# First output piece with its relu terms ahead of its weight-product terms, and state sums that VectorE decays kept in PSUM

## The chip, the cores and the metric

The kernel runs on one core of one Trainium2 chip. The metric is the device time of one execution in microseconds (us), taken as the median over runs. Engines are called TensorE (PE in the profile, PEld for its weight loads), VectorE (DVE), ScalarE (ACT), GpSimd (POOL) and SyncE (SP, which issues all DMAs here).

## The reference

Two stages. A gated linear attention over 4 batches, 8 heads, 768 tokens, head dimension 48:

```
f = 1 / (1 + exp(-f_logit))
for t in range(S):
    state = f[t, :, None] * state + outer(k[t], v[t])      # 48 x 48 per batch and head
    y[t] = q[t] @ state
```

Then, with x the 3072 x 384 matrix of all y rows (heads side by side), a maxout layer: `out = maximum(x @ w1, x @ w2) @ w_out`, with w1 and w2 of 384 x 1024 and w_out of 1024 x 384. Inputs and output are f32.

## The kernel before, in words

**Tiling.** The 3072 rows are cut into 12 windows s = 0 to 11 of 256 tokens; window s belongs to batch s % 4 and is that batch's window number s // 4. A window lies on 128 partitions with two neighbouring tokens (even and odd) on each. Its lower and upper 64 partitions are its halves h = 0 and 1, of 128 tokens each. The recurrence is worked out chunk by chunk: inside a half by a masked product of decayed q and k, and from half to half by a 48 x 48 state per head, kept in bf16 in the tiles `st0` to `st3` (one per batch).

**The steps of a window.** E, F and G (ScalarE) turn f_logit into logs of the gates; e (line 202) adds even and odd; C (lines 206, 209) makes cumulative sums on TensorE; X and Z (ScalarE, lines 216, 221) make `inv` and `dec` from them; i, j, K and Q (lines 225, 229, 236, 239) decay k and q; V casts v; t and u transpose k and q on TensorE (line 256) and U copies them to SBUF (`trs`); A (line 273) makes the products and m masks them; S (line 313) adds what the previous states give and y (lines 313, 341) what the window itself gives; Y casts the result to `xT`. z (line 329) reads two elements, so that what follows is ordered after S.

**The state.** D (line 357) sums k times v of each half into one PSUM bank per half (`sadd`, 128 x 192 f32). Step n (lines 370 to 375) handles a half that has a state before it by adding that state to the sums, into the SBUF f32 tile `tmp_s` (three buffers in rotation); step N (line 378) then multiplies `tmp_s` by the decay (a slice of `dec`, spread over 48 columns) and writes the new state. A half with no state before it (half 0 of windows 0 to 3) takes one multiplication straight from PSUM (line 375). N runs on GpSimd for 14 of its 16 uses, and on VectorE for half 0 of window 5 (N5.0) and of window 10 (N10.0).

**The maxout layer.** It is computed as relu(x (w1 - w2)) w_out + x (w2 w_out). `wd` is w1 - w2 (line 482); `m2` is the product w2 w_out, in three row blocks: TensorE products wm (line 472), stored by wn (line 476, helper line 103). d (line 396) multiplies `xT` by `wd` into PSUM, r (lines 405, 407) takes the relu into `gT`, and o (lines 412 to 421) makes one output piece of 128 rows (the even or the odd tokens of a window; in the last window the odd piece is cut in two): first three terms `xT` x `m2` (line 417), then eight terms `gT` x `wo` (line 420), accumulated in one PSUM bank. b copies a piece to SBUF; O and P store.

**The order of the work** is written out by hand in the string `ORDER` (lines 20 to 54): one word per step, with the window, the piece or half, the engine (a ScalarE, v VectorE, p GpSimd, s SyncE) and the PSUM bank after @. Every engine takes its words in that order; semaphores between engines follow from what the steps read and write. The words around the change:

```
... wm0@7 E2 r0.1v@4 ... wm2@6 E3 e2p wn0v@7 wm1@4 ... j2v wn2a@6 e3p C2@7 wn1v@4 d1.3@1 ... i2v o0.0@6 Z2 K2v
... Q2v t2@4 r1.1a@0 D2@2 Lf4s@10 u2@4 ...
... A5.0@0 D5@2 X7 N4.1p z4 o3.0@5 n5.0v Z7 N5.0v E6 Q7p Lq8s@2
n5.1v m5.0v@0 E8 S5@2 y4 b3.0a@5 ... A5.1@0 F6 o3.1@5 m5.1v@0 Y4a@6 e6p
... D10@5 A10.1@0 z11 n10.0v y11 N10.0v m10.1v@0 S10@2 o9.1@5 ...
```

The first output piece is o0.0. The states that the change touches are made by n5.0v and N5.0v, which S5 reads, and n10.0v and N10.0v, which S10 reads.

Of the kernel before, what the change touches and what calls it, by code (L numbers as in the profile page):

```python
# [11 lines left out]
F32 = mybir.dt.float32  # L12
# [7 lines left out]
ORDER = """  # L20
# [37 lines left out]
def kernel(  # L58
# [14 lines left out]
    nc = tc.nc  # L73
    B, H, S, D = q.shape
    C = 128
# [3 lines left out]
    NP = H // 2  # L79
# [3 lines left out]
    FG = d_ff // C  # L83
    KT = HD // C
    n_s = nw * B
    places = [(x, h, x * DP - h * D) for x in range(2 * KT) for h in range(H)
              if x * DP < (h + 1) * D and h * D < (x + 1) * DP]

    consts = ctx.enter_context(tc.tile_pool(name="consts", bufs=1))
    inp = ctx.enter_context(tc.tile_pool(name="inp", bufs=1))  # L90
    work = ctx.enter_context(tc.tile_pool(name="work", bufs=2))
# [85 lines left out]
    wo = consts.tile([C, FG, HD], BF16, name="wo")  # L177
    m2 = consts.tile([C, KT, HD], BF16, name="m2")
# [8 lines left out]
    gate, ell, one, cum, inv, dec, tr, at_b, at, states, sadd, tmps = ({} for _ in range(12))  # L187
# [99 lines left out]
    def has_state(s, h):  # L287
        return s >= B or h > 0

    def state_before(s, h):  # L290
        return states[s][:, 0] if h else states[s - B][:, 1]
# [70 lines left out]
    def decay(s, h):  # L362
        return dec[s][:, HD:].rearrange("p (j h) -> p j h", h=2)[:, :, h:h + 1].to_broadcast([C, NP, D])

    def state_of(s):
        if s not in states:
            states[s] = pad(f"st{s % B}", s)
        return states[s]

    def step_n(s, h):  # L370
        if has_state(s, h):
            tmps[s, h] = work.tile([C, NP, D], F32, name="tmp_s", tag="tmp_s", bufs=3)
            nc.vector.tensor_add(tmps[s, h], sadd[s][h][:, :, 0:D], state_before(s, h)[:, 1::2, :])  # L373
        else:
            nc.vector.tensor_mul(state_of(s)[:, h, 1::2, :], sadd[s][h][:, :, 0:D], decay(s, h))

# [4 lines left out]
    xT, gT, obs = {}, {}, {}  # L381
# [6 lines left out]
    def x_flat(s):  # L388
        return xT[s].rearrange("p k a h t -> p k (a h t)")
# [19 lines left out]
    def piece(g, i):  # L409
        return (i, slice(0, HD)) if i == 0 or g < n_s - 1 else (1, (slice(0, 2 * C), slice(2 * C, HD))[i - 1])  # L410

    def step_o(g, i, b):
        par, m = piece(g, i)
        cols = slice(par * C, (par + 1) * C)
        ps = banks[:, b, m]
        for kt in range(KT):
            nc.tensor.matmul(out=ps, lhsT=x_flat(g)[:, kt, cols], rhs=m2[:, kt, m],  # L417
                             start=(kt == 0), stop=False)
        for ff in range(FG):
            nc.tensor.matmul(out=ps, lhsT=gT[g][:, ff, cols], rhs=wo[:, ff, m],  # L420
                             start=False, stop=(ff == FG - 1))

    def step_b(g, i, e, b):
        par, m = piece(g, i)
# [54 lines left out]
    def subtract(q, e):  # L479
# [20 lines left out]
        "Y": lambda s, e, b: step_Y(s, e, b),  # L500
        "D": lambda s, e, b: step_D(s, b),
        "n": lambda s, i, e, b: step_n(s, i), "N": lambda s, i, e, b: step_N(s, i, e),
        "d": lambda s, i, e, b: step_d(s, i, b), "r": lambda s, i, e, b: step_r(s, i, e, b),
        "o": lambda s, i, e, b: step_o(s, i, b), "b": lambda s, i, e, b: step_b(s, i, e, b),
        "O": lambda s, e, b: step_O(s), "P": lambda s, i, e, b: step_P(s, i, e),
        "wc": lambda i, e, b: cast_w2(i, e), "wt": lambda i, e, b: transpose_w2(i, b),
# [1 line left out]
        "wm": lambda i, e, b: m2_product(i, b), "wn": lambda i, e, b: store_m2(i, e, b),  # L508
        "ws": lambda i, e, b: subtract(i, e),
    }  # L510
    for word in ORDER.split():
        key, of, e, b = re.fullmatch(r"([A-Za-z]+)([0-9.]+)([avps]?)@?([0-9]*)", word).groups()
        steps[key](*map(int, of.split(".")), e, int(b or 0))

# [29 lines left out]
```

## Time and profile before

| | us |
|---|---|
| median of 3 runs | 141.15 |
| lowest, highest | 140.92, 141.65 |
| the profiled execution | 141.12 |
| its span, first to last instruction | 139.3 |

| engine | busy us | share of the span |
|---|---|---|
| TensorE | 122.4 | 88% |
| VectorE | 99.6 | 72% |
| ScalarE | 83.1 | 60% |
| GpSimd | 56.6 | 41% |

The granted TensorE clock was 1.000 over the span. Matmuls overlap their neighbours in these records: a group's printed end is modelled and lies up to 0.2 us behind the start of the next group where TensorE runs without a stop. The printed idle time before an instruction is counted from that end. A wait is put down to the engine and line whose semaphore came last.

### The profile page before, as it was taken

Reading aid. Unit: us, or ns where it says so; the run is one execution under the profiler, and the core shown is the slowest. Engines: PE = TensorE matmul, PEld = TensorE weight load, DVE = VectorE, ACT = ScalarE, POOL = GpSimd, SP = SyncE. Lnnn points to the kernel's source line nnn. Section 1 sums busy time; section 2 is a strip of 40 time slices with the busy share of each in tenths; the row PEclk is TensorE's granted clock in tenths of the full one; section 3 lists DMA queues with packets and bytes.
Section 4 is the critical chain, followed back from the end, with each engine's and each line's share of the span. In section 5 each row is a group of like instructions: output and inputs, shape, how many; then the busy total and the mean of one; then the engine's idle time right before and its main releaser. Section 6 shows DMA issues by size and latency. Waiting matters only on the chain.

```text
span 139.3 us, 5772 instructions
## 1 busy us (share of the span) xinstructions
PE 122.4 (88%) x2575; PEld 91.6 (66%) x2575; DVE 99.6 (72%) x155; ACT 83.1 (60%) x119; POOL 56.6 (41%) x64
## 2 busy tenths in 40 slices
PE   0026699999899999996999999999999999999991
PEld 0024677876567788665688657886678876778670
DVE  5778968756988787789778686967957689643130
ACT  3646464769677679796578687978126470404400
POOL 7604519526188795736601382530860501000000
PEclk9999999999999999999999999999999999999999
DMA  4999999999999999999999999891113000032014
GB/s 112 271 261 264 374 386 378 334 257 238 274 266 239 256 268 274 273 263 253 292 316 273 244 260 292 239 319 50 59 59 118 0 5 7 5 132 98 3 53 169
DMA packets 54617, 28.68 MB, mean 206 GB/s; under 512 B 50240, under 2 KB 51648, under 8 KB 54592
## 3 DMA queue, kind: packets, MB, share of 16 engines
q1 hardware_dynamic: 54592, 28.32, 76.7%
q8 instruction: 20, 0.33, 1.0%
q14 instruction: 5, 0.04, 0.1%
HBM read 23.59 MB, written 4.72 MB: 203 GB/s over the span
## 4 chain that ended last, share of the span: by engine, by line
PE 79%; DMA 9%; DVE 3%; POOL 3%; SPq 2%; ACT 2%; issue 1%; DVEq 0%; POOLq 0%
PE banks L396 23%; PE banks L420 21%; PE banks L417 9%; DMA slots<-in_moe_w_dram 6%; PE banks L341 5%; PE banks L256 4%; PE banks L273 4%; PE banks L313 4%; PE banks L472 3%; DMA slots<-in_f_logit_dram 3%; POOL wd L482 3%; PE banks L357 2%; PE banks L206 2%; DVE st L378 1%; SPq L114 1%; SPq L125 1%
## 5 line engine op out<-in xcount | busy, mean ns | idle before, releaser
L420 PE MATMUL banks<-wo,gT 128*128 128x384 bf16 (+2 forms) x200 | 35.3, 320 | 0.0
L396 PE MATMUL banks<-xT,wd 128*128 128x256 bf16 x288 | 34.6, 274 | 0.3 <-POOL wd L482 0.3
L281 DVE TENSOR_TENSOR at_m<-banks,mask 128x1024 bf16<-128x1024 f32 x24 | 28.7, 1218 | 6.0 <-PE banks L273 6.0
L396 PEld LDWEIGHTS <-wd 128*128 128x128 bf16 x288 | 27.3, 98 | 4.5 <-POOL wd L482 0.6
L420 PEld LDWEIGHTS <-gT 128*128 128x128 bf16 x200 | 19.3, 98 | 12.0
L405 ACT ACTIVATE gT<-banks 128x1024 bf16<-128x1024 f32 x16 | 16.0, 1022 | 9.5 <-PE banks L396 9.2
L239 POOL TENSOR_TENSOR qp<-slots,dec 128x768 bf16<-128x768 f32 x8 | 15.1, 1888 | 11.4 <-ACT dec L221 6.0
L103 ACT COPY ob<-banks 128x384 f32<-128x384 f32 (+2 forms) x18 | 9.0, 501 | 16.8 <-PE banks L420 14.1
L378 POOL TENSOR_TENSOR st<-tmp_s,dec 128x192 bf16<-128x192 f32 x14 | 7.9, 566 | 23.6 <-DVE tmp_s L373 21.4
L417 PE MATMUL banks<-m,xT 128*128 128x384 bf16 (+2 forms) x75 | 16.1, 321 | 0.4 <-DVE m L103 0.4
L407 DVE TENSOR_SCALAR gT<-banks 128x1024 bf16<-128x1024 f32 x8 | 9.7, 1222 | 5.7 <-PE banks L396 5.3
L191 ACT ACTIVATE gate<-slots 128x768 f32<-128x768 f32 x12 | 10.0, 845 | 4.6 <-DMA slots<-in_f_logit_dram 4.6
L103 DVE COPY ob<-banks 128x384 f32<-128x384 f32 (+2 forms) x11 | 5.9, 542 | 8.5 <-PE banks L420 8.1
L103 DVE COPY trs<-banks 128x2048 bf16<-128x2048 bf16 x8 | 9.7, 1220 | 3.0 <-PE banks L256 3.0
L341 PE MATMUL banks<-at_m,vb 64*64 64x128 bf16 x576 | 11.7, 224 | 0.0
L103 ACT CAST xT<-banks 128x768 bf16<-128x768 f32 x8 | 6.4, 798 | 8.8 <-PE banks L341 8.7
L225 POOL TENSOR_TENSOR slots<-slots,one 128x384 f32<-128x384 f32 x7 | 7.6, 1084 | 9.8 <-ACT one L199 6.4
L273 PE MATMUL banks<-trs 48*64 48x128 bf16 x384 | 9.6, 234 | 1.3 <-DVE trs L103 1.3
L313 PE MATMUL banks<-trs,st 48*64 48x128 bf16 x240 | 8.7, 227 | 2.2 <-DVE look L329 1.1
L195 ACT ACTIVATE ell<-gate 128x768 f32<-128x768 f32 x12 | 10.1, 843 | 0.6
L236 DVE TENSOR_TENSOR kp<-slots,inv 128x768 bf16<-128x768 f32 x9 | 8.6, 963 | 2.6 <-issue 1.4
L206 PE MATMUL banks<-e,u_inc 128*128 128x384 bf16 x12 | 4.3, 356 | 6.8 <-DVE e L202 6.8
(64 smaller groups left out, 180.1 us busy)
## 6 DMA issues: line engine op xcount, KB each, us to landing
slots<-in_f_logit_dram SPq DMA_DIRECT2D x12, 384.0 KB, 6.3
slots<-in_k_dram SPq DMA_DIRECT2D x12, 384.0 KB, 6.4
slots<-in_q_dram SPq DMA_DIRECT2D x12, 384.0 KB, 6.2
slots<-in_v_dram SPq DMA_DIRECT2D x12, 384.0 KB, 6.1
out_dram<-ob SPq DMA_DIRECT2D x11, 384.0 KB, 5.4
slots<-in_moe_w_dram SPq DMA_DIRECT2D x4, 768.0 KB, 9.1
slots<-in_moe_w_out_dram SPq DMA_DIRECT2D x2, 768.0 KB, 13.6
out_dram<-ob SPq DMA_DIRECT2D x1, 192.0 KB, 1.9
```

The costliest lines, as they stand in the source:

```text
L103: (nc.scalar.copy if e == "a" else engines[e].tensor_copy)(out, in_)
L191: nc.scalar.activation(flat(gate[s]), flat(loaded[s]["f"]), AF.Exp, bias=0.0, scale=-1.0)
L195: nc.scalar.activation(flat(ell[s]), flat(gate[s]), AF.Ln, bias=1.0, scale=1.0)
L239: engines[e].tensor_mul(pad("qp", s)[:, :, :, 0:D], by_parity(loaded[s]["q"]), both(dec[s][:, 0:HD].rearrange("p (h d) -> p h d", h=H)))
L273: nc.tensor.matmul(out=ps[h * HC:(h + 1) * HC, j % 2, par, :], lhsT=t[rows, h, 0, j, par, :], rhs=t[rows, h, 1, j].rearrange("p a t -> p ( ...
L281: nc.vector.tensor_mul(at[s][:, jj].rearrange("p r j a t -> p (r j) (a t)"), banks[:, b:b + 2, :].rearrange("p r (j x) -> p (r j) x", j=2) ...
L313: nc.tensor.matmul(out=ys[s][h][cols, kt, :], lhsT=window(state_before(s, h)[rows], head // 2, off), rhs=tr[s][rows, h, 1, head // 2].rear ...
L341: nc.tensor.matmul(out=ys[s][h][cols, kt, :], lhsT=window(vb[rows, par], head, off), rhs=m[rows, head // 4, head % 2, head // 2 % 2, par, ...
L396: nc.tensor.matmul(out=ps[:, f, :], lhsT=wd[:, kt, ff * C:(ff + 1) * C], rhs=x_flat(g)[:, kt, :], start=(kt == 0), stop=(kt == KT - 1))
L405: nc.scalar.activation(dst, src, AF.Relu)
L417: nc.tensor.matmul(out=ps, lhsT=x_flat(g)[:, kt, cols], rhs=m2[:, kt, m], start=(kt == 0), stop=False)
L420: nc.tensor.matmul(out=ps, lhsT=gT[g][:, ff, cols], rhs=wo[:, ff, m], start=False, stop=(ff == FG - 1))
```

## The change

In the output piece that comes first in `ORDER` (o0.0) the eight relu terms are issued before the three `m2` terms; all other pieces keep their order. Where N runs on VectorE (N5.0 and N10.0), step n writes its sum over the sums in PSUM, instead of into `tmp_s`, and N multiplies from there. `ORDER` itself, and so the order of the steps on each engine, is the same. The rotation of the three `tmp_s` buffers skips these two uses.

```diff
+    words = ORDER.split()
...
     def step_n(s, h):
         if has_state(s, h):
-            tmps[s, h] = work.tile([C, NP, D], F32, name="tmp_s", tag="tmp_s", bufs=3)
-            nc.vector.tensor_add(tmps[s, h], sadd[s][h][:, :, 0:D], state_before(s, h)[:, 1::2, :])
+            sums = sadd[s][h][:, :, 0:D]
+            tmps[s, h] = sums if f"N{s}.{h}v" in words else work.tile([C, NP, D], F32, name="tmp_s", tag="tmp_s", bufs=3)
+            nc.vector.tensor_add(tmps[s, h], sums, state_before(s, h)[:, 1::2, :])
...
+    first_o = tuple(map(int, re.search(r"\bo(\d+\.\d+)", ORDER).group(1).split(".")))
+
     def step_o(g, i, b):
...
-        for kt in range(KT):
-            nc.tensor.matmul(out=ps, lhsT=x_flat(g)[:, kt, cols], rhs=m2[:, kt, m],
-                             start=(kt == 0), stop=False)
-        for ff in range(FG):
-            nc.tensor.matmul(out=ps, lhsT=gT[g][:, ff, cols], rhs=wo[:, ff, m],
-                             start=False, stop=(ff == FG - 1))
+        terms = [(x_flat(g)[:, kt, cols], m2[:, kt, m]) for kt in range(KT)]
+        relu = [(gT[g][:, ff, cols], wo[:, ff, m]) for ff in range(FG)]
+        terms = relu + terms if (g, i) == first_o else terms + relu
+        for n, (x, w) in enumerate(terms):
+            nc.tensor.matmul(out=ps, lhsT=x, rhs=w, start=(n == 0), stop=(n == KT + FG - 1))
```

More of the change, by code (lines that the diff above doesn't have):

```diff
@@ L510 @@
     }
-    for word in ORDER.split():
+    for word in words:
         key, of, e, b = re.fullmatch(r"([A-Za-z]+)([0-9.]+)([avps]?)@?([0-9]*)", word).groups()
```

## The prediction

> **What bounds the kernel now.** I read the page first, then the waits of TensorE, then the chain of waits around the two places that the change touches, and last the timeline there.
>
> ```profile
> PE 122.4 (88%) x2575; PEld 91.6 (66%) x2575; DVE 99.6 (72%) x155; ACT 83.1 (60%) x119; POOL 56.6 (41%) x64
> ...
> PE 79%; DMA 9%; DVE 3%; POOL 3%; SPq 2%; ACT 2%; issue 1%; DVEq 0%; POOLq 0%
> ```
>
> The chain that ended last is 79% TensorE, and in time order it holds nothing but TensorE from 64.64 us to 136.24 us. A microsecond gained on TensorE before 64.64 therefore comes out at the end, unless something that does not move with TensorE is late behind it. TensorE's list of waits is short, and after 24 us only two entries of it are left, both at places of this change:
>
> ```profile
> PE banks L313 <- DVE tmp_s L373: 1.0, 1, 1.0
> PE banks L417 <- DVE m L103: 0.4, 1, 0.4
> ```
>
> The first is S5, which waits for window 5's state; the second is the first output piece, which waits for the second block of `m2`. The chain around S5, as start, length, what:
>
> ```profile
> 61.45 0.32 PE banks L357 x32
> ...
> 61.83 0.37 DVE tmp_s L373
> ...
> 62.23 1.88 DVE st L378
> ...
> 64.23 0.37 DVE tmp_s L373
> 64.60 0.04 issue
> 64.64 0.53 PE banks L313 x24
> ```
>
> The sums D5 (L357) end, VectorE adds (n5.0, 0.37), decays (N5.0, 1.88), adds the other half (n5.1, 0.37), and only then S5 starts. N5.0 is the odd one: line 378 on VectorE has two uses, 357 and 1873 ns.
>
> **Why 1.88 us.** The timeline shows what ran beside such instructions (start, length, engine, line):
>
> ```profile
> 62.07 1.81 POOL L239 TENSOR_TENSOR qp<-slots,dec 128x768 bf16<-128x768 f32 x1 [2.23 <-ACT dec L221]
> ...
> 62.23 1.87 DVE L378 TENSOR_TENSOR st<-tmp_s,dec 128x192 bf16<-128x192 f32 x1
> ...
> 88.32 1.82 POOL L239 TENSOR_TENSOR qp<-slots,dec 128x768 bf16<-128x768 f32 x1 [3.82 <-ACT dec L221]
> ...
> 88.97 1.58 DVE L225 TENSOR_TENSOR slots<-slots,one 128x384 f32<-128x384 f32 x1
> ...
> 79.70 1.82 POOL L239 TENSOR_TENSOR qp<-slots,dec 128x768 bf16<-128x768 f32 x1
> ...
> 80.20 0.35 DVE L373 TENSOR_TENSOR tmp_s<-banks,st 128x192 f32<-128x192 f32 x1
> ```
>
> N5.0 began 0.16 us after GpSimd's Q7 and ended at 64.10, 0.22 after Q7 (63.88). Line 225 in the second pair takes 0.55 us alone (its median) and ended 0.41 after GpSimd's instruction; line 229 at 33.50 (1.33 long, 0.55 alone) also ended 0.41 after one, and at 65.64 (0.71 long) 0.42 after one. In all four the end lies 0.13 to 0.14 us short of the instruction's own length behind GpSimd's end: VectorE stood still until GpSimd was through. All four read two operands from SBUF. The third pair reads one from PSUM and one from SBUF, lies wholly inside a GpSimd instruction, and takes 0.35 as always. The form that N5.0 gets, PSUM times `dec` into a state, is line 375's: four uses, 346 to 356 ns; the one at 43.54 to 43.89 lies across two GpSimd instructions (43.26 to 43.77 and 43.73 to 44.74) and is no longer.
>
> **Part 1, N5.0 from PSUM.** N5.0 falls from 1.87 to 0.35 us: 1.52 less on VectorE. n5.1 then ends at 64.59 - 1.52 = 63.07, and S5 could start 0.05 later (the step from VectorE's end to TensorE's start at S5 and at the first piece), at 63.12. What is late next is TensorE itself: the output piece o3.0 ends at 62.13 + 1.46 = 63.59, and a step behind an output piece starts 0.08 before that printed end (S11 at 118.96, piece ended 119.04), at 63.51. So S5 moves from 64.64 to 63.51: **-1.13 us**, and 0.39 us of VectorE's gain is cover that is not used.
>
> Does the rest follow? In y4, nothing: its inputs were done by 61.44. A5.1 needs m5.0, now done at 65.72 - 1.52 = 64.20, and would start at 64.64. C6 started at 68.58 and would at 67.45; its e6 on GpSimd, tied to ScalarE's F6 and not to TensorE, ends at 65.93. GpSimd's cast of window 7's v waits for a load that lands at 67.87 whatever happens; VectorE's K6, right behind, can lose some 0.1 to 0.4 us to that cast, and t6, t7 and u6 stand at least 0.67 us behind what they read. The other loads land 2.1 us or more before their first use, except window 9's v, whose sums D9 come 7.8 us after its cast. The tail from 136.2 on is stores and stays.
>
> **Part 2, N10.0.** It met no GpSimd instruction (357 ns) and becomes line 375's form, 350 ns: nothing. It has almost no cover: it ends at 120.43, S10 starts at 120.48, and TensorE's y11 would have let it start at 120.64 - 0.08 = 120.56. No new wait comes of keeping the banks longer: S5 (banks 2 and 3) waits for N5.0 anyway, and o9.1, which writes bank 5 of window 10's sums, stands behind S10, which waits for N10.0. The `tmp_s` rotation shifts; each use finds its buffer's last reader done at least 3 us before.
>
> **Unknown: an add that writes PSUM.** No row of VectorE writes PSUM. From below: line 373 into SBUF takes 353 ns and line 375 350, so a gain is at most some 0.01. From above: if reading and writing one bank take turns, the add pays its 192 elements twice; by lines 281 and 373, (1218 - 353) / (1024 - 192) = 1.04 ns per element, that is +0.20. At S5 that is inside the 0.39; at S10 it costs 0.20 - 0.08 = 0.12. I take nothing, by line 373, which has the same reads and element count.
>
> [...]
>
> **Part 3, the first piece.** Its `m2` terms wait for wn1, which ends at 35.30; relu inputs were done at 31.68. With relu terms first, eight at 1.30 us, the `m2` terms come after 35.8, so the 0.43 us stop goes, and the piece ends at about 36.7. But what follows waits for VectorE, which doesn't move:
>
> ```profile
> 35.35 0.48 PE L417 MATMUL banks<-m,xT 128*128 128x384 bf16 x2 [0.43 <-DVE m L103]
> ...
> 36.74 0.95 DVE L239 TENSOR_TENSOR qp<-slots,dec 128x768 bf16<-128x768 f32 x1
> ...
> 37.78 0.41 PE L256 MATMUL banks<-ident,qp 64*128 64x64 bf16 x16
> ```
>
> t2 needs K2, done at 36.83, so it starts at 36.88 (was 37.07). u2 needs Q2, done at 37.69, so it starts at 37.74, was 37.78. **-0.04 us**; 0.39 of the 0.43 is spent waiting for VectorE two steps on.
>
> **Sum.** -1.13 + 0 - 0.04 = -1.17. The profiled execution, 141.12 (span 139.3 and 1.8 around it), becomes 139.95. It lies 0.03 under the median of 141.15, so the forecast is 141.15 - 1.17 = **140.0 us**, -0.8%. What a measurement of this kernel can tell from no change is about 0.5% (0.7 us).
>
> **Rivals.**
> *N5.0 stays blocked.* It still reads `dec` from SBUF; if that one read is enough to be held up by Q7, the time is 141.1. For it: only a short overlap was seen for exactly this form. Against: the add inside Q8, at its usual length, and line 375 at 43.54. Chance 0.09.
> *The gain is given back.* A VectorE instruction with two SBUF operands that now meets GpSimd differently: line 225 at 88.97 lost 1.03 so, of which 0.87 is covered (K9 ended 91.61, t9 started 92.53). Losses of 0.2 to 0.8 are possible: 140.2 to 140.8. Against: GpSimd's Q and VectorE's work beside it are both set by TensorE and shift together. Chance 0.11, a quarter of it over 140.44.
> *Slower: in-place PSUM work costs VectorE more.* Let x be what add and multiplication together take more. S5 loses x - 0.39, S10 x - 0.08. The change breaks even at 2x - 0.47 = 1.17, x = 0.82, and is 0.7 us slower from x = 1.17. If each of the four runs of 48 elements paid a fixed cost like the smallest VectorE row (line 329, 151 ns for two elements) in both instructions, x = 8 x 0.151 = 1.21: 139.95 + 0.82 + 1.13 = 141.9. Against: lines 373 and 375 read the same four runs from PSUM in 350. Chance 0.05.
> *The first piece keeps its whole 0.43.* It needs K2 and Q2 0.4 us earlier, which nothing provides; 139.6. Chance 0.05.
>
> **Numbers.** Forecast 0.70, given back 0.11, still blocked 0.09, slower 0.05, more 0.05. Faster by over 0.5%: 0.70 + 0.05 + 0.08 = 0.83; within 0.5%: 0.09 + 0.03 = 0.12; slower 0.05. Range: 139.5 (first piece's full gain, and the spread of the median) to 140.7 (most of the given-back case, the 0.12 of the add); it leaves out still blocked, slower and a little more, under 0.2.
>
> **What would show it.** Right: line 378 gone from the long rows, its VectorE form `st<-banks,dec` at 0.35 beside Q7; no idle time before S5; y10's and S10's starts earlier by the same 1.2. At the first piece, no idle before the `m2` terms but some 0.2 before t2, and u2 at the same time as before. Wrong: N5.0 still over 1 us, an add into `banks` clearly over 0.36, S10 waiting for the state, or new idle time on TensorE between 64 and 136 us.

## The result, and the profile after

| | before | changed | ratio, 95% interval |
|---|---|---|---|
| median, 8 runs each | 141.07 us | 140.16 us | 0.993 (0.990 to 0.996) |
| the profiled execution | 141.12 us | 139.52 us | |
| its span | 139.3 us | 137.7 us | |

The change is faster by 0.9 us (0.6 to 1.4 by the interval), which is under 1%; 140.0 was forecast. The two profiled executions lie 1.6 us apart, and not all of that is the change: runs of one kernel spread over more than a microsecond (the changed one from 139.52 to 140.64), and the profiled one is its fastest. The places below tell the two apart.

The page of the changed kernel, its parts 1 and 4 (lines of the file are moved by 2 to 4: its 375 is line 373 of before, 380 is 378, 240 is 239, 314 is 313, 257 is 256; both kinds of terms of an output piece are now line 424):

```profile
PE 122.3 (89%) x2575; PEld 91.6 (66%) x2575; DVE 98.6 (72%) x155; ACT 82.9 (60%) x119; POOL 56.3 (41%) x64
...
PE 72%; DMA 12%; DVE 8%; ACT 4%; issue 1%; DVEq 0%
```

VectorE's busy time fell by 1.0 us although it has the same 155 instructions; N5.0 alone became 1.5 shorter, and among the instructions that now meet GpSimd differently K (9.3 us in all instead of 8.6) and i (4.2 instead of 3.8) took more, j (7.9 instead of 8.6) less. TensorE's share of the chain fell from 79% to 72% because the chain now runs, ahead of u2, through VectorE (j2, wn1, i2, K2, Q2) and ScalarE to a load of f_logit. TensorE's waits after:

```profile
PE banks L207 <- DVE e L203: 6.8, 1, 6.8
PE banks L358 <- ACT vb L104: 2.5, 1, 2.5
PE banks L274 <- DVE trs L104: 1.3, 1, 1.3
PE banks L314 <- DVE look L330: 1.1, 1, 1.1
PE banks L358 <- issue: 0.4, 1, 0.4
PE banks L398 <- POOL wd L485: 0.2, 1, 0.2
```

The two entries at the places of the change, `DVE tmp_s` (1.0) and `DVE m` (0.4), are gone; the 1.1 left on line 314 is an early one. The chain around S5 after:

```profile
61.11 0.25 PE banks L358 x32
61.36 1.89 PE banks L424 x11
63.25 0.46 PE banks L314 x24
63.71 0.67 PE banks L342 x48
```

D5, o3.0, S5, y4: TensorE alone, without a step through VectorE. The timeline of the same stretch shows why:

```profile
61.49 0.37 DVE L375 TENSOR_TENSOR banks<-banks,st 128x192 f32<-128x192 f32 x1 [0.39 <-PE banks L358]
...
61.73 1.82 POOL L240 TENSOR_TENSOR qp<-slots,dec 128x768 bf16<-128x768 f32 x1 [2.22 <-ACT dec L222]
...
61.89 0.36 DVE L380 TENSOR_TENSOR st<-banks,dec 128x192 bf16<-128x192 f32 x1
...
62.35 0.36 DVE L375 TENSOR_TENSOR tmp_s<-banks,st 128x192 f32<-128x192 f32 x1
...
63.18 0.53 PE L314 MATMUL banks<-trs,st 48*64 48x128 bf16 x24
```

Q7 began 0.16 us ahead of N5.0, exactly as before, and N5.0 (second DVE line) ran inside it in 0.36 us instead of 1.87.

Set against the same steps of before, TensorE's steps show two jumps. From u2 on the changed run is 0.34 us ahead; at S5 this becomes 1.46 (1.12 more), at A5.1 1.56, and 1.58 at the last output piece. From S5 to the start of that piece both need the same time within 0.12 us (70.81 and 70.69), so nothing is given back later. The 1.24 that comes at S5 and A5.1 (1.58 less 0.34) is one matter, the 0.34 at u2 another:

```profile
33.49 0.56 DVE L230 SCALAR_TENSOR_TENSOR slots<-gate,slots 128x384 f32<-128x384 f32 x1 [1.25 <-ACT ell L196]
...
33.53 1.38 POOL L203 TENSOR_TENSOR e<-ell 128x384 bf16<-128x384 f32 x1 [0.61 <-ACT ell L196]
...
34.69 1.46 PE L424 MATMUL banks<-wo,gT 128*128 128x384 bf16 x8
...
35.99 0.65 PE L424 MATMUL banks<-m,xT 128*128 128x384 bf16 x3
...
36.43 0.94 DVE L240 TENSOR_TENSOR qp<-slots,dec 128x768 bf16<-128x768 f32 x1
...
37.44 0.41 PE L257 MATMUL banks<-ident,qp 64*128 64x64 bf16 x16
```

The first two lines are VectorE's j2 and GpSimd's e3. Before, e3 began 0.08 us ahead of j2, took 1.00, and j2 took 1.33. Here j2 began 0.04 us ahead, took 0.56, and it was e3 that took 1.38. VectorE was through with wn1 0.8 us earlier, so K2 and Q2, for which t2 and u2 wait, were earlier too. Nothing in the change touches j2 or e3. So the question for the experiments was whether the 0.34 belongs to the first output piece or to that race.

### The profile page after: what moved, and what is told of

Same layout as the page of the kernel before. It is cut to its first block, busy times and chain, and to the rows that moved or that the text cites. A ratio compares the mean times of both kernels' runs of the same rounds, so it can differ in the third digit from the quotient of the medians.

```text
span 137.7 us, 5772 instructions
## 1 busy us (share of the span) xinstructions
PE 122.3 (89%) x2575; PEld 91.6 (66%) x2575; DVE 98.6 (72%) x155; ACT 82.9 (60%) x119; POOL 56.3 (41%) x64
## 4 chain that ended last, share of the span: by engine, by line
PE 72%; DMA 12%; DVE 8%; ACT 4%; issue 1%; DVEq 0%
PE banks L424 31%; PE banks L398 20%; DMA slots<-in_f_logit_dram 12%; PE banks L342 6%; PE banks L274 4%; PE banks L257 4%; PE banks L314 4%; PE banks L358 2%; ACT ell L196 2%; ACT gate L192 2%; DVE at_m L282 2%; PE banks L207 2%; DVE kp L237 1%; DVE qp L240 1%; DVE trs L104 1%; DVE slots L230 1%
## 5 line engine op out<-in xcount | busy, mean ns | idle before, releaser
L237 DVE TENSOR_TENSOR kp<-slots,inv 128x768 bf16<-128x768 f32 x9 | 9.3, 1037 | 2.5 <-issue 1.3
L342 PEld LDWEIGHTS <-vb 64*64 64x64 bf16 x576 | 10.0, 111 | 0.0
```

What stands on the lines that cost most here:

```text
L237: engines[e].tensor_mul(pad("kp", s)[:, :, :, 0:D], by_parity(loaded[s]["k"]), both(inv[s]))
L342: nc.tensor.matmul(out=ys[s][h][cols, kt, :], lhsT=window(vb[rows, par], head, off), rhs=m[rows, head // 4, head % 2, head // 2 % 2, par, ...
```

## The experiments

**The state part alone.** The changed kernel with the old order of terms:

```diff
-        terms = relu + terms if (g, i) == first_o else terms + relu
+        terms = terms + relu
```

> Only the state part: N5.0 and N10.0 decay sums kept in PSUM, the first output piece keeps its old order. Theory (VectorE stood still behind GpSimd's Q7 because N5.0 read two operands from SBUF): N5.0 takes 0.36 us beside Q7, S5 has no idle time before it, and TensorE is 1.25 us earlier from A5.1 on (1.12 at S5, 0.13 more because A5.1 no longer waits for m5.0); ratio to before about 0.991. Rival (most of the measured gain is the first output piece): less than 0.4 us gained, ratio above 0.997.

Measured: 140.62 us beside 141.38 for before, ratio 0.994 (0.991 to 0.996). Timeline:

```profile
62.06 1.82 POOL L240 TENSOR_TENSOR qp<-slots,dec 128x768 bf16<-128x768 f32 x1 [2.22 <-ACT dec L222]
...
62.22 0.36 DVE L380 TENSOR_TENSOR st<-banks,dec 128x192 bf16<-128x192 f32 x1
...
63.51 0.53 PE L314 MATMUL banks<-trs,st 48*64 48x128 bf16 x24
```

This run reached u2 within 0.02 us of before (37.76 against 37.78), so it is the clean comparison: S5 at 63.51 instead of 64.64, 1.13 earlier (63.51 was forecast), A5.1 1.23, the last piece 1.25. GpSimd's e3 went ahead of j2 in both. Alone, the state part gives a gain as large as that of the whole change, within the intervals (0.991 to 0.996 and 0.990 to 0.996); the rival falls.

**The first output piece alone.** The changed kernel with `tmp_s` for all sums:

```diff
-            tmps[s, h] = sums if f"N{s}.{h}v" in words else work.tile([C, NP, D], F32, name="tmp_s", tag="tmp_s", bufs=3)
+            tmps[s, h] = work.tile([C, NP, D], F32, name="tmp_s", tag="tmp_s", bufs=3)
```

> Only the first output piece: relu terms first, sums of the state in tmp_s as before. Theory (t2 and u2 wait for VectorE's K2 and Q2, which do not move): the 0.43 us idle time before the piece's weight-product terms goes and comes back before t2 and u2, ratio 1.000, at most 0.05 us gained. Rival (the piece brings 0.3 to 0.4 us, as the profiled run of the changed kernel could be read, where u2 started 0.34 us earlier): ratio about 0.997.

Measured: 141.28 us beside 141.38, ratio 1.000 (0.997 to 1.002). Timeline:

```profile
33.37 1.00 POOL L203 TENSOR_TENSOR e<-ell 128x384 bf16<-128x384 f32 x1 [0.61 <-ACT ell L196]
33.39 1.39 DVE L230 SCALAR_TENSOR_TENSOR slots<-gate,slots 128x384 f32<-128x384 f32 x1 [0.99 <-ACT ell L196]
...
36.83 0.29 PEld L257 LDWEIGHTS <-kp 64*128 64x128 bf16 x16 [0.42 <-DVE kp L237]
...
37.70 0.29 PEld L257 LDWEIGHTS <-qp 64*128 64x128 bf16 x16 [0.19 <-DVE qp L240]
37.71 0.41 PE L257 MATMUL banks<-ident,qp 64*128 64x64 bf16 x16
```

The stop inside the piece is gone, and t2 and u2 now wait for K2 and Q2 (the idle times in brackets). u2 starts at 37.71 against 37.78, of which 0.04 is VectorE's own (Q2 began at 36.70 against 36.74). Here e3 began first again, and j2 took 1.39. Only 0.03 is the piece's.

**Q7 later, nothing of the change.** The kernel before, with two ScalarE steps turned so that `dec` of window 7 is ready later:

```diff
-... n5.0v Z7 N5.0v E6 Q7p ...
+... n5.0v E6 N5.0v Z7 Q7p ...
```

> The kernel before, with nothing of the change; only ScalarE's order is turned so that Z7 comes after E6, which lets GpSimd's Q7 start near 63.0 us, after N5.0 (which still reads tmp_s and dec from SBUF). Theory (N5.0 was only long because Q7 had begun first): N5.0 takes 0.36 us, S5 starts without idle time, and the gain is that of the state part alone, about 1.1 to 1.25 us (ratio about 0.991). Rival (a sum read back from SBUF is slow at this place by itself, whatever GpSimd does): N5.0 stays at 1.87 us and the ratio at 1.000.

Measured: 140.22 us beside 141.38, ratio 0.992 (0.989 to 0.995). Timeline:

```profile
62.11 0.36 DVE L378 TENSOR_TENSOR st<-tmp_s,dec 128x192 bf16<-128x192 f32 x1
...
62.68 1.82 POOL L239 TENSOR_TENSOR qp<-slots,dec 128x768 bf16<-128x768 f32 x1 [2.95 <-ACT dec L221]
...
63.41 0.53 PE L313 MATMUL banks<-trs,st 48*64 48x128 bf16 x24
...
64.01 0.91 DVE L229 SCALAR_TENSOR_TENSOR slots<-gate,slots 128x384 f32<-128x384 f32 x1
```

N5.0 still reads both operands from SBUF and takes 0.36, because Q7 is not there; S5 started 1.89 us behind the start of o3.0 instead of 3.01, the same gain of 1.12. So neither `tmp_s` nor line 378 was slow: standing behind Q7 was. Q7's price went to j6 (last line, 0.91 for 0.55, ended 0.42 behind Q7), where it is covered.

**N5.0 twice, and five times.** The changed kernel, to see what S5 hangs on now (N5.0 repeated, the same state written; the edit is that for one more, with 5 in place of 2 for four more):

```diff
-        engines[e].tensor_mul(state_of(s)[:, h, 1::2, :], tmps.pop((s, h)), decay(s, h))
+        sums = tmps.pop((s, h))
+        for x in range(2 if (s, h) == (5, 0) else 1):
+            engines[e].tensor_mul(state_of(s)[:, h, 1::2, :], sums, decay(s, h))
```

> The changed kernel with the multiplication N5.0 done twice (the same result into the same state). Theory (behind the change S5 waits for TensorE, and VectorE's chain n5.0, N5.0, n5.1 has 0.42 us of cover: n5.1 ends at 62.71 and S5 starts at 63.18 in the changed kernel's profile): the chain grows by 0.3 to 0.4 us, S5 shows no idle time and starts right behind the output piece o3.0; at most 0.1 us is lost at A5.1. Rival (S5 still hangs on VectorE): S5 is later by the full 0.3 to 0.4 us.

> The changed kernel with the multiplication N5.0 done five times. Theory: VectorE's chain grows by 1.1 to 1.6 us, of which 0.42 is covered, so S5 stands idle 0.7 to 1.2 us, as before the change, and nearly all of the state part's gain is gone (ratio to before 0.996 to 1.001). Rival (the time that N5.0 takes does not set S5): ratio stays at 0.993.

Measured with one more (a single run of 139.99 us, which allows no verdict on the time): VectorE's chain grew by 0.40 us, n5.1 ended at 63.48, and S5 started at 63.55 without idle time, right behind o3.0 (first line). A5.1 lost 0.08: it stood behind m5.0, which ended at 64.61. With four more the chain grew by 1.57, and TensorE's wait was back (second line):

```profile
63.55 0.53 PE L314 MATMUL banks<-trs,st 48*64 48x128 bf16 x24
...
64.22 0.53 PE L314 MATMUL banks<-trs,st 48*64 48x128 bf16 x24 [1.08 <-DVE tmp_s L375]
```

Measured 141.38 us beside 141.34 for before (23 runs beside the last four experiments), ratio 1.000 (0.998 to 1.002): with the 1.92 us of five multiplications in place of the 1.87 of the blocked one, the gain is gone. Of the 1.57, S5 lost 1.15 against the start of o3.0; the other 0.42 is the cover, forecast at 0.39.

**The race of j2 and e3 decided.** One ScalarE copy goes ahead of F3, so that e3 comes later; first on the kernel before, then on the changed one:

```diff
-... F3 j2v wn2a@6 e3p ...
+... wn2a@6 F3 j2v e3p ...
```

> The kernel before; only ScalarE's copy of the third block of m2 (wn2) goes ahead of F3, which makes GpSimd's e3 start near 34.0 us, behind VectorE's j2 (33.5). In the profiled run of before e3 began 0.08 us ahead of j2 and j2 took 1.33 us, in that of the changed kernel j2 began 0.04 ahead and took 0.56. Theory (which of the two begins first changes from run to run, and is worth the 0.34 us by which u2 was earlier in the changed kernel's profile): j2 takes 0.55, u2 starts near 37.4, and the median is 0.1 to 0.4 us under that of before with a smaller spread. Rival (the 0.34 came from the first output piece): u2 stays at 37.8 and the median does not move.

> The changed kernel with ScalarE's copy of the third block of m2 ahead of F3, so that VectorE's j2 always begins before GpSimd's e3. Theory (the order of j2 and e3 changes from run to run and is worth some 0.3 us where j2 loses): j2 takes 0.55 us and u2 starts near 37.4; the median is 0 to 0.3 us under that of the changed kernel run beside it, ratio to before 0.989 to 0.993. Rival (no effect that lasts): same ratio as the changed kernel.

> The changed kernel once more, beside the others. Ratio to before 0.991 to 0.995. In its profile j2 either begins before e3 (0.56 us long, u2 near 37.4) or behind it (1.3 us, u2 near 37.75), and S5 starts right behind o3.0 either way.

On the kernel before:

```profile
33.43 0.56 DVE L229 SCALAR_TENSOR_TENSOR slots<-gate,slots 128x384 f32<-128x384 f32 x1 [1.24 <-DMA slots<-in_k_dram]
...
37.45 0.41 PE L256 MATMUL banks<-ident,qp 64*128 64x64 bf16 x16
```

j2 took 0.56 and u2 started 0.33 earlier, as in the changed kernel's profile and without any part of the change. So the 0.34 is the race's. The traces of the other runs agree, with the one exception below: where j2 went first u2 started at 37.32 to 37.45, where e3 did at 37.66 to 37.80. But the median, 141.17 beside 141.38, has ratio 0.999 (0.996 to 1.002): the expected gain of 0.1 to 0.4 us is not shown, nor a clearly smaller spread (140.69 to 142.16, beside 140.82 to 142.49). The profiled run shows how the gain was lost there:

```profile
51.93 0.32 PEld L357 LDWEIGHTS <-kp 64*64 64x64 bf16 x29
52.48 0.11 PEld L357 LDWEIGHTS <-kp 64*64 64x64 bf16 x3 [0.23 <-issue]
```

In the middle of D4 TensorE's weight loads stop, for no semaphore that the profile shows; D4 took 0.77 us instead of 0.44, and the 0.33 was gone. The same stop, at the same 30th weight load of D4, stands in the next two runs below (0.64 and 0.45 us of idle time), and one inside d5.3 in the first-piece run (0.41). In all four the stop ended 1.24 to 1.53 us after the end of a 16 KB packet of the instruction queue (q8 in part 3 of the page). Where the packet ended 1.5 us or more ahead of these loads (at D4 1.9 in the profile of before, 1.8 in that of the changed kernel) there was no stop, but three traces passed one of these places without a stop at 1.35 to 1.49, so the ranges overlap. No experiment was made on it, and the cause is not shown.

On the changed kernel the same edit gave 140.13 us, ratio 0.990 (0.987 to 0.994), and the changed kernel beside it 140.11, ratio 0.994 (0.991 to 0.997). The intervals overlap, and the two medians (which the ratios are not the quotients of) lie 0.02 us apart: inconclusive. The expectation for u2 in that run missed (37.84, not 37.4): j2 won the race (0.56), but wn1 began 0.35 us later than in the changed kernel's profile, later C4 waited 0.6 us for GpSimd, and D4 stopped as told. That wait of C4 is the same block the other way: GpSimd's e4 (46.76) started just behind VectorE's j4, which reads two operands from SBUF, and took 1.40 instead of 1.00. In the repeated changed kernel e3 won, j2 took 1.40 and u2 started at 37.74; S5 stood right behind o3.0, as expected.

## Why the prediction was right, point by point

- **What made N5.0 long: right.** It stood behind Q7. Moved away from Q7 it took 0.36 us from SBUF; taken from PSUM it took 0.36 us inside Q7. Beside Q7, with both operands from SBUF, it had taken 1.87, while Q7 kept its 1.81. Of j2 and e3 too the one that began later is the long one: j2 1.33 us where e3 began 0.08 ahead, e3 1.38 where j2 began 0.04 ahead.
- **Part 1, S5: right to 0.01 us** (-1.13 forecast, 63.51; the clean run has 63.51). The cover behind it was put at 0.39; n5.1 ends at 62.71 and S5 starts at 63.18 in the changed kernel's profile, which with the 0.05 of the step leaves 0.42; 0.40 more work was hidden from S5, and of 1.57 more 0.42.
- **A term was left out.** A5.1 was taken to move with S5. Before, it had itself waited for m5.0 (ended 65.72, A5.1 at 65.77), which the change also frees: A5.1 gained 0.10 more than S5, and from y5 on the gain is 1.24. The forecast of -1.13 was short by 0.11.
- **"Does the rest follow?": right in the time, with less room than it said.** From S5 to the last piece the time is the same within 0.12 us. But window 7's v did not land at 67.87 whatever happens: in the changed kernel's profile it landed at 68.72. So the cast of it met K7 and not K6, for which 0.1 to 0.4 us had been forecast, and K7 lost 0.63 (1.58 instead of 0.95). TensorE did not notice, but u6 started only 0.18 us behind the end of Q6, VectorE's next step, where before there were 0.72. That nothing was given back here was in part luck.
- **Part 2, N10.0 and the add that writes PSUM: right.** The add takes 366 ns into PSUM and 353 into `tmp_s`, +0.013 against a range of -0.01 to +0.20; the multiplication takes 358 ns from PSUM against 357 from SBUF. S10 comes 0.01 us later behind D10, and the next piece, o9.1, no later. The slower rival, which needs 0.82 us per pair, has 0.01.
- **Part 3, the first piece: right.** Its stop goes and comes back before t2 and u2; -0.04 forecast, 0.03 to 0.07 in the trace, ratio 1.000.
- **The size.** The sum was -1.17; the medians give 0.9, with 0.6 to 1.4 inside the interval. The traces show 1.24 at S5 and A5.1. Both fit the interval. Whether the 0.3 between them is more than the spread of the runs (33 of before, beside the first four experiments, lie between 140.82 and 142.49 us) stays open: behind S5 the only thing given back in any trace is the 0.3 of the stop in d5.3, in a run without the state part. What was not weighed is that one profiled execution can be 0.3 us off through a race of two engines, and as much again or more through a stop like that in D4 (0.23 to 0.64).

## What to carry to other kernels

An instruction with two durations far apart in one profile is worth more than its sum: set each long one against what GpSimd runs at that moment, and see whether its end follows the end of that. Two ways out were measured here, to take one operand from PSUM and to move the other engine's instruction. Both gave the same (S5 1.89 us behind the start of o3.0 instead of 3.01) and cost next to nothing: 13 ns in the add that writes PSUM, or 0.36 us of j6, which was covered. And a stop that goes is only worth the time until the next wait for something that does not move; look two steps on before you count it.

## What the runs showed of the hardware

- The block went both ways, and a lead of 0.02 us was enough: with e3 ahead by that much, j2 took 1.39 us instead of 0.56 (the first-piece run), by 0.08 us 1.33 (the kernel before); with j2 ahead by 0.04 us, e3 took 1.38 instead of 1.00 (the changed kernel). The two profiled executions of the changed kernel, the same code, lie on either side.
- The blocked instruction, on either engine, ended its own length, less 0.13 to 0.15 us, behind the end of the other: in the four cases of the kernel before, and also for j6 behind Q7 (0.42 for 0.55), K7 behind the cast of window 7's v (0.81 for 0.95) and GpSimd's e3 behind j2 (0.86 for 1.00).
- An in-place add on PSUM took VectorE 13 ns more than one into SBUF (366 against 353 ns for 128x192 f32, two and 14 uses in the changed kernel's profile).
- TensorE stopped for 0.23 to 0.64 us inside a row of weight loads without a semaphore (four of ten traces), each time until 1.24 to 1.53 us after a packet of the instruction queue; that the packet is the cause is not shown. The 20 such packets of the profile of before took 0.88 to 1.50 us each, those of the changed kernel's 0.88 to 1.26.
